# Spreading loads and preparation over the iterations, and moving TensorE transposes behind PV, in a fused attention and FFN kernel

## The chip, the cores and the metric

The kernel runs on one core of one Trainium2 chip. The metric is device microseconds (us) of one execution; a median of several runs is quoted with its range. A profile is one execution; its span, from the first to the last instruction, is about 1.8 us shorter than the time reported for the same run. Before the change the time was 451.42 us (median of 3 runs, 450.83 to 452.55).

## The reference, cut to what matters

```python
# q, k, v: [8, 8, 1152, 64]; two neighbouring queries are averaged: 576 rows
q_pool = q.reshape(B, H, S // 2, 2, D).mean(axis=3)
scores = np.matmul(q_pool, k.transpose(0, 1, 3, 2)) / np.sqrt(D)
attn   = softmax(scores)                       # over 1152 keys
x      = (attn @ v).transpose(0, 2, 1, 3).reshape(4608, 512)
out    = ((x @ w1) * (x @ w2)) @ w3 @ w_out    # d_ff = 1024
```

The kernel multiplies `w3 @ w_out` once, to a matrix T, and then runs the FFN in nine units of 512 tokens.

## The kernel before

Heads are handled in 32 *pairs*. A pair has 9 x 576 columns of scores, cut into chunks of 512 that run on across pairs; the loop makes two chunks in each of 162 *iterations*, so a pair takes 5.06 of them. In an iteration TensorE makes the scores of two chunks, ScalarE their exponentials, TensorE the products with v (PV) of the chunks before, and then *filler*: matmuls of T or of FFN units whose tokens are ready, until a running account (`busy`) of TensorE time reaches `due`. Two FFN units are left for a *tail* behind the loop.

Each pair has to be prepared: loads of k, q and v with a cast (queue of GpSimd), three copies on VectorE (pooled q, reordered k, v), and a transpose of k and q. The first eight pairs are transposed by TensorE, the others by DMA transposes, because in the beginning the DMA engines are full of loads.

```python
def load(P):      load_k(P); load_q(P); load_v(P)       # kst, vst: 4 buffers; qst: 3 pairs of two

def prep_stage(P):                                      # pairs 1 to 7, VectorE, in one go
    pool_q(P)
    kcs[P] = ab.tile(...); nc.vector.tensor_copy(out=kcs[P]..., in_=kst.pop(P))
    copy_v(P)

def prep_pe(P):                                         # 18 transposes, two PSUM tiles of tag "ff"
    t2 = psum.tile([128, 1024], FP16, tag="ff", bufs=2); t1 = psum.tile(..., tag="ff", bufs=2)
    ...                                                 # q and k[8] into t2, k[0..7] into t1
    nc.vector.tensor_copy(out=qT[P]..., in_=t2[:, 128:704])
    if P == 0: nc.scalar.copy(out=kT[P][:, 0:8]..., in_=t1)
    else:      nc.vector.tensor_copy(out=kT[P][:, 0:8]..., in_=t1)
    nc.vector.tensor_copy(out=kT[P][:, 8], in_=t2[:, 0:128])

def prep_dma(P):                                        # pairs 8 to 31: k, its transpose,
    ...                                                 # q, its transpose, v: in one go

def normalize(P):                                       # frees po, which has ONE buffer
    acc = po.pop(P)...; nc.vector.reciprocal(...); nc.vector.tensor_tensor(out=xn, ...)
    nc.sync.dma_start_transpose(out=xT..., in_=xn...)

load_q(0); load_k(0); ...; load_v(0); load(1); load(2)
load_w3(0); load_w(wosb, moe_w_out); load(3); load_w3(1)
...
for it in range(162):
    if it in T_AT: filler.append(gen_T(...))            # T_AT = (8, 14)
    scores(2*it); expo(2*it); scores(2*it+1); expo(2*it+1)
    at = it * 2 * CH / PAIR                             # position, in pairs
    if staged < 8 and at >= staged - 0.8:
        prep_stage(staged); ...                         # and one or two of the loads that wait
    if prepped < 32 and at >= prepped - (0.5 if prepped < 8 else 1.6):
        if prepped < 8: fill(0, settle=True); prep_pe(prepped)
        else:           prep_dma(prepped); load(loaded); ...
    for J, i in ready: attend(J, i)                     # PV
    if last: normalize(...)
    fill(due)
```

`settle=True` finishes the open accumulation group of the filler, because transposes and filler share the two `ff` tiles.

The softmax here doesn't subtract the row's maximum and nothing guards it: scores larger than these inputs give would overflow.

Of the kernel before, what the change touches and what calls it, by code (L numbers as in the profile page):

```python
# [8 lines left out]
FP16 = mybir.dt.float16  # L9
# [6 lines left out]
NJ = 9  # L16
# [7 lines left out]
def kernel(  # L24
# [11 lines left out]
    nc = tc.nc  # L36
    B, H, S, D = q.shape
# [5 lines left out]
    NP = B * H // 2  # L43
    SCL = 16.0
    NPE = 8
    T_AT = (8, 14)

    T_MM, T_TR, T_SC, T_AV = 0.216, 0.06, 0.63, 0.061
    PACE0, PACE1 = 2.2, 2.19
    SCALE = 0.5 * float(D) ** -0.5  # L50

# [2 lines left out]
    ab = ctx.enter_context(tc.tile_pool(name="ab", bufs=4))  # L54
    ffp = ctx.enter_context(tc.tile_pool(name="ffp", bufs=2))
    psum = ctx.enter_context(
        tc.tile_pool(name="psum", bufs=1, space=bass.MemoryType.PSUM))

    xT = const.tile([128, NC, NT], FP16)
    w1sb = const.tile([128, NC, dff], FP16)  # L60
    w2sb = const.tile([128, NC, dff], FP16)
# [6 lines left out]
    ident = const.tile([128, 128], FP16)  # L68
# [7 lines left out]
    kst, vst, qst, kT, qT, qps = {}, {}, {}, {}, {}, {}  # L76

    def load_q(P):
        if P % 2 == 0:
            qst[P // 2] = stage.tile([128, 2, 18, D], FP16, tag="qst", bufs=3, name="qst")  # L80
        b, h0 = P // 4, 2 * (P % 4)
        o = 64 * (P % 2)
        nc.gpsimd.dma_start(
            out=qst[P // 2][o:o + 64].rearrange("p u t d -> p u (t d)"),
            in_=q[b, h0:h0 + 2].rearrange("u (p t) d -> p u (t d)", t=18))

    def load_k(P):
        b, h0 = P // 4, 2 * (P % 4)
        kst[P] = stage.tile([128, 2, NJ, D], FP16, tag="kst", name="kst")
        nc.gpsimd.dma_start(  # L90
            out=kst[P].rearrange("p u j d -> p u (j d)"),
            in_=k[b, h0:h0 + 2].rearrange("u (p j) d -> p u (j d)", j=NJ))

    def load_v(P):
        b, h0 = P // 4, 2 * (P % 4)
        vst[P] = stage.tile([128, 2, NJ, D], FP16, tag="vst", name="vst")
        nc.gpsimd.dma_start(  # L97
            out=vst[P].rearrange("p u j d -> p u (j d)"),
            in_=v[b, h0:h0 + 2].rearrange("u (p j) d -> p u (j d)", j=NJ))

    def load(P):
        if P < NP:
            load_k(P)
            load_q(P)
            load_v(P)

    def pool_q(P):

        pp, o = P // 2, 64 * (P % 2)
        if P % 2 == 0:  # L110
            qps[pp] = ab.tile([128, NJ, 2, D], FP16, tag="qp", bufs=2, name="qp")
        if P < NPE:
            r = slice(o, o + 64)
        elif P % 2 == 0:
            r = slice(0, 128)
        else:
            return
        src = qst[pp][r].rearrange("p u (c two) d -> p u c two d", two=2)
        nc.vector.tensor_tensor(
            out=qps[pp][r].rearrange("p c u d -> p u c d"),  # L120
            in0=src[:, :, :, 0, :], in1=src[:, :, :, 1, :], op=ALU.add)

    def new_kq(P):
        kT[P] = ab.tile([128, NJ, 128], FP16, tag="kT", bufs=3, name="kT")
        qT[P] = ab.tile([128, NJ, 64], FP16, tag="qT", bufs=3, name="qT")

    def copy_v(P):
        nc.vector.tensor_copy(out=vts[P % 4][:, :, :, 0:D], in_=vst.pop(P))

    def prep_dma(P):  # L130

        pp, o = P // 2, 64 * (P % 2)
        new_kq(P)
        kc = ab.tile([128, NJ, 2, D], FP16, tag="kc", bufs=2, name="kc")
        nc.vector.tensor_copy(out=kc.rearrange("p j u d -> p u j d"), in_=kst.pop(P))  # L135
        nc.sync.dma_start_transpose(out=kT[P], in_=kc.rearrange("p j u d -> p (j u d)"))
        pool_q(P)
        nc.sync.dma_start_transpose(
            out=qT[P], in_=qps[pp][o:o + 64].rearrange("p c u d -> p (c u d)"))
        copy_v(P)  # L140

    kcs = {}

    def prep_stage(P):

        pool_q(P)
        kcs[P] = ab.tile([128, NJ, 2, D], FP16, tag="kc", bufs=2, name="kc")
        nc.vector.tensor_copy(out=kcs[P].rearrange("p j u d -> p u j d"), in_=kst.pop(P))
        copy_v(P)

    def prep_pe(P):
        pp, o = P // 2, 64 * (P % 2)
        new_kq(P)
        kc = kcs.pop(P)
        t2 = psum.tile([128, 1024], FP16, tag="ff", bufs=2, name="t2")
        t1 = psum.tile([128, 1024], FP16, tag="ff", bufs=2, name="t1")
        for c in range(NJ):
            nc.tensor.transpose(t2[:, 128 + 64 * c:192 + 64 * c],
                                qps[pp][o:o + 64, c].rearrange("p u d -> p (u d)"),
                                ident[o:o + 64, o:o + 64])  # L160
        for j in (8, 0, 1, 2, 3, 4, 5, 6, 7):
            dst = t1[:, 128 * j:128 * j + 128] if j < 8 else t2[:, 0:128]
            nc.tensor.transpose(dst, kc[:, j].rearrange("p u d -> p (u d)"), ident)
        nc.vector.tensor_copy(out=qT[P].rearrange("p c f -> p (c f)"), in_=t2[:, 128:704])
        if P == 0:
            nc.scalar.copy(out=kT[P][:, 0:8].rearrange("p j f -> p (j f)"), in_=t1)
        else:
            nc.vector.tensor_copy(out=kT[P][:, 0:8].rearrange("p j f -> p (j f)"), in_=t1)  # L168
        nc.vector.tensor_copy(out=kT[P][:, 8], in_=t2[:, 0:128])


    psc = {}
# [60 lines left out]
    def load_w3(i):  # L233
        t = ffp.tile([128, 4, dff], FP16, tag="g", name="w3h")
        nc.gpsimd.dma_start(
            out=t, in_=moe_w3.rearrange("(c p) f -> p c f", p=128)[:, 4 * i:4 * i + 4])
        w3h.append(t)

    def load_w(dst, src):
        nc.gpsimd.dma_start(out=dst, in_=src.rearrange("(c p) f -> p c f", p=128))  # L240
# [31 lines left out]
    def gen_ffn(t, tail):  # L272
# [25 lines left out]
        for i in range(4):  # L298
# [13 lines left out]
            for s in range(2):  # L312
# [13 lines left out]
        out=ident, in_=ident, compare_op=ALU.not_equal, fill=1.0,  # L326
        base=0, channel_multiplier=1, pattern=[[-1, 128]])
    load_v(0)
    load(1)
    load(2)  # L330
    load_w3(0)
    load_w(wosb, moe_w_out)
    load(3)
    load_w3(1)
    waiting = [lambda: load(4), lambda: load_w(w1sb, moe_w1), lambda: load_w(w2sb, moe_w2),
               lambda: load(5), lambda: load(6)]
    loaded, staged, prepped = 7, 1, 1
    prep_stage(0)
    prep_pe(0)

    n_units = NT // 512
    filler = []
    next_unit = 0
    busy = due = 0.0
# [4 lines left out]
    def fill(until, settle=False):  # L349

        nonlocal busy, whole
        while filler and (not whole if settle else busy < until):
            try:
                cost, whole = next(filler[0])
                busy += cost
            except StopIteration:
                filler.pop(0)

    for it in range(NIT):
        if it in T_AT:  # L360
            filler.append(gen_T(T_AT.index(it)))

        while next_unit < n_units:
            last_b = (512 * (next_unit + 1) - 1) // SQ
            if (last_b + 1) * 4 * PAIR + 3 * 2 * CH > it * 2 * CH:
                break
            filler.append(gen_ffn(next_unit, False))
            next_unit += 1
        scores(2 * it)
        expo(2 * it)  # L370
        scores(2 * it + 1)
        expo(2 * it + 1)
        busy += T_SC
        due = (due if filler else busy - T_SC) + (PACE0 if it < 20 else PACE1)
        at = it * 2 * CH / PAIR
        if staged < NPE and at >= staged - 0.8:
            prep_stage(staged)
            staged += 1
            if waiting:
                waiting.pop(0)()  # L380
                if waiting:
                    waiting.pop(0)()
            else:
                load(loaded)
                loaded += 1
        lead = 0.5 if prepped < NPE else 1.6
        if prepped < NP and at >= prepped - lead:
            if prepped < NPE:
                fill(0, settle=True)
                prep_pe(prepped)  # L390
            else:
                prep_dma(prepped)
                load(loaded)
                loaded += 1
            prepped += 1
        ready = [b for b in blocks[nb:nb + 40]
                 if b[0] * SQ + min(128 * b[1] + 128, SQ) <= 2 * it * CH]

        last = [n for n, (J, i) in enumerate(ready) if J % NJ == NJ - 1 and i == 4]
        if last:  # L400
            ready = ready[:last[0] + 1]
        busy += T_AV * len(ready)
        for J, i in ready:
            attend(J, i)
        if last:
            normalize(ready[-1][0] // NJ)
        nb += len(ready)
        fill(due)
    for J, i in blocks[nb:]:
        attend(J, i)  # L410
    normalize(NP - 1)
# [37 lines left out]
```

## Time and profile before

| | before |
|---|---|
| time, median of 3 runs | 451.42 us |
| span of the profiled execution | 446.9 us |
| TensorE / ScalarE / VectorE busy | 94% / 74% / 44% |
| iterations 0-7, 41-160: us each | 2.0, 2.27 |
| iteration 40 | 8.34 us |
| TensorE idle in iteration 40 | 4.73 us |

The start of an iteration is read as the start of its first exponential (324 exponentials, two for each iteration). The page's first part (engine: us busy, share of the span, instructions) and a line of its fourth (the chain of work that ended last):

```profile
PE 418.3 (94%) x5168; PEld 222.5 (50%) x5168; DVE 198.2 (44%) x347; ACT 329.8 (74%) x350; POOL 69.9 (16%) x107
...
PE 82%; DMA 5%; ACT 4%; DVE 4%; issue 3%; SPq 1%; POOL 0%; ACTq 0%; DVEq 0%; POOLq 0%
```

TensorE (PE) is the limit almost everywhere. The stretches of 10 us show where it is not: each line has the busy time and the instructions of each engine, the granted TensorE clock (the share of full speed that TensorE was allowed), the mean busy share of the DMA engines, and what they moved. The busy share adds up the time of all packets and divides it by 16 engines; over 1, packets overlap on an engine.

```profile
core 0: us, PE busy (x) PEld busy (x) DVE busy (x) ACT busy (x) POOL busy (x), PEclk, DMA share, GB/s
10.00:20.00 10.00, 8.37 (x123) 5.45 (x123) 2.96 (x7) 8.62 (x10) 4.29 (x7) 1.00 1.16 207
20.00:30.00 10.00, 7.57 (x137) 5.45 (x137) 4.64 (x10) 8.30 (x9) 1.47 (x2) 1.00 1.27 204
100.00:110.00 10.00, 10.00 (x126) 5.06 (x124) 4.56 (x9) 8.76 (x10) 2.03 (x3) 1.00 1.39 126
110.00:120.00 10.00, 5.27 (x49) 2.54 (x49) 1.15 (x3) 3.38 (x5) 0.00 (x0) 0.83 1.25 131
200.00:210.00 10.00, 9.97 (x143) 5.45 (x140) 3.82 (x8) 8.60 (x9) 2.03 (x3) 1.00 0.73 104
```

The last line is the steady state: TensorE without a gap, ScalarE (ACT) at 8.6 of 10 us. From 110 to 120 us TensorE loses almost half its time and part of its clock. The timeline of TensorE there (start, us, engine, line, operation, out<-in, count, and in brackets the idle time before it with what ended it):

```profile
109.91 0.39 PE L187 MATMUL psc<-qT,kT 64*128 64x512 f16 x2
115.03 0.61 PE L187 MATMUL psc<-qT,kT 64*128 64x512 f16 x2 [4.73 <-DMA qT<-qp]
```

and the line of the chain of waits for the same place (start, us, what):

```profile
98.94 15.96 DMA qT<-qp
```

The scores of pair 8, the first that is transposed by DMA, wait for its q. That transpose was issued at 98.94 us and took 15.96 us to land. The trace's clock record has 0.5 of the full clock for 3.41 us from 114.64 on.

### The profile page before, as it was taken

The numbers are of one execution on the slowest core, as the hardware profiler recorded it, in microseconds if no ns is written. First come the engines' busy times: TensorE is split into PE (matmuls) and PEld (weight loads), VectorE is DVE, ScalarE is ACT, GpSimd is POOL, SyncE is SP. The second block draws the span as 40 slices with busy tenths as digits, with TensorE's granted clock in tenths as the row PEclk, the third lists the DMA queues.
The fourth block names the chain that finished last, engine by engine and source line by source line (L and its number), as shares of the span: only waits on it lengthen the run. The fifth ranks groups of instructions, "written<-read, shape, count | busy, mean of one in ns | idle before, by whom it ended". The sixth has DMA issues, their size and how long they took to land.

```text
span 446.9 us, 12036 instructions
## 1 busy us (share of the span) xinstructions
PE 418.3 (94%) x5168; PEld 222.5 (50%) x5168; DVE 198.2 (44%) x347; ACT 329.8 (74%) x350; POOL 69.9 (16%) x107
## 2 busy tenths in 40 slices
PE   2889898998799999999999999999999999989995
PEld 1556454554355555555555555545555555544442
DVE  2245454574234553554445445544554444433130
ACT  2977776778488888888888888878888888823332
POOL 7312140131101121111111111111100000000000
PEclk9999999999899999999999999999999999999999
DMA  8999999669999999999899999979882460131304
GB/s 132 209 188 206 207 183 194 100 99 122 135 196 141 136 135 223 135 155 117 163 169 130 142 175 166 137 110 182 163 151 56 98 101 19 15 73 36 92 4 94
DMA packets 94468, 59.11 MB, mean 132 GB/s; under 512 B 66256, under 2 KB 83664, under 8 KB 94416
## 3 DMA queue, kind: packets, MB, share of 16 engines
q0 software_dynamic: 25168, 33.56, 50.4%
q1 hardware_dynamic: 69248, 24.79, 37.3%
q8 instruction: 40, 0.66, 0.6%
q14 instruction: 12, 0.10, 0.1%
HBM read 67.11 MB, written 9.44 MB: 171 GB/s over the span
## 4 chain that ended last, share of the span: by engine, by line
PE 82%; DMA 5%; ACT 4%; DVE 4%; issue 3%; SPq 1%; POOL 0%; ACTq 0%; DVEq 0%; POOLq 0%
PE po L206 20%; PE psc L187 19%; PE pb L291 13%; PE pa L278 13%; PE pp L301 12%; ACT er L193 4%; DMA qT<-qp 4%; PE pT L265 3%; DMA vst<-in_v_dram 1%; DVE xn L218 1%; DVE kT L168 1%; PE w3t L250 1%; DMA out_dram<-osb 1%; DVE T_73 L269 0%; DVE osb L310 0%
## 5 line engine op out<-in xcount | busy, mean ns | idle before, releaser
L193 ACT ACTIVATE er<-psc 128x1024 f16<-128x1024 f32 x324 | 313.4, 1022 | 70.8 <-PE psc L187 68.0
L187 PE MATMUL psc<-qT,kT 64*128 64x512 f16 (+7 forms) x1152 | 108.8, 289 | 11.3 <-DMA qT<-qp 4.7
L206 PEld LDWEIGHTS <-er 128*128 128x128 f16 x2880 | 97.3, 97 | 35.1 <-issue 31.8
L187 PEld LDWEIGHTS <-kT 64*128 64x128 f16 x1152 | 44.2, 94 | 95.4 <-issue 83.7
L291 PE MATMUL pb<-xT,w2sb 128*128 128x512 f16 x288 | 79.7, 379 | 2.4 <-DVE osb L310 1.3
L278 PE MATMUL pa<-xT,w1sb 128*128 128x512 f16 x288 | 79.1, 379 | 1.2 <-DVE asb L287 0.7
L296 DVE TENSOR_TENSOR gT<-pb,asb 128x512 f16<-128x512 f32 x72 | 49.6, 689 | 63.5 <-PE pb L291 63.0
L301 PE MATMUL pp<-T_73,gT 128*128 128x512 f16 x288 | 70.8, 382 | 0.0
L287 DVE COPY asb<-pa 128x512 f32<-128x512 f32 x56 | 38.5, 688 | 46.9 <-PE pa L278 46.9
L90 POOL DMA_DIRECT2D kst<-in_k_dram x32 | 23.0, 718 | 217.1 <-DVE kc L135 173.3
L310 DVE TENSOR_SCALAR osb<-pp 128x512 f32<-128x512 f32 x28 | 19.3, 690 | 53.5 <-PE pp L301 51.1
L301 PEld LDWEIGHTS <-gT 128*128 128x128 f16 x288 | 25.5, 98 | 24.4 <-issue 0.5
L278 PEld LDWEIGHTS <-w1sb 128*128 128x128 f16 x288 | 25.8, 97 | 23.8 <-issue 0.7
L291 PEld LDWEIGHTS <-w2sb 128*128 128x128 f16 x288 | 25.4, 97 | 23.6 <-issue 1.6
L206 PE MATMUL po<-vt_77,er 128*128 128x65 f16 x720 | 29.7, 195 | 0.0
L206 PE MATMUL po<-vt_80,er 128*128 128x65 f16 x720 | 29.4, 195 | 0.1
L206 PE MATMUL po<-vt_78,er 128*128 128x65 f16 x720 | 28.7, 193 | 0.0
L206 PE MATMUL po<-vt_79,er 128*128 128x65 f16 x720 | 28.7, 193 | 0.0
L285 ACT COPY asb<-pa 128x512 f32<-128x512 f32 x16 | 9.4, 586 | 24.4 <-PE pa L278 24.4
L218 DVE TENSOR_TENSOR xn<-po,rz 128x640 f16<-128x640 f32 x32 | 26.4, 824 | 1.3 <-DVE rz L216 0.2
L97 POOL DMA_DIRECT2D vst<-in_v_dram x32 | 23.3, 729 | 17.4 <-DMA w3h<-in_moe_w_dram 5.3
L216 DVE RECIPROCAL rz<-po 128x10 f32<-128x10 f32 x32 | 7.1, 221 | 37.6 <-PE po L206 37.5
(80 smaller groups left out, 147.7 us busy)
## 6 DMA issues: line engine op xcount, KB each, us to landing
qst<-in_q_dram POOLq DMA_DIRECT2D x32, 288.0 KB, 7.8
kst<-in_k_dram POOLq DMA_DIRECT2D x32, 288.0 KB, 5.5
vst<-in_v_dram POOLq DMA_DIRECT2D x32, 288.0 KB, 9.4
out_dram<-osb SPq DMA_DIRECT2D x72, 128.0 KB, 3.4
w3h<-in_moe_w_dram POOLq DMA_DIRECT2D x2, 1024.0 KB, 20.4
wosb<-in_moe_w_out_dram POOLq DMA_DIRECT2D x1, 1024.0 KB, 19.2
xT<-xn SPq DMA_TRANSPOSE x64, 3.8
w1sb<-in_moe_w_dram POOLq DMA_DIRECT2D x1, 1024.0 KB, 21.6
```

Of the source, the lines that this page charges most:

```text
L90: nc.gpsimd.dma_start(out=kst[P].rearrange("p u j d -> p u (j d)"), in_=k[b, h0:h0 + 2].rearrange("u (p j) d -> p u (j d)", j=NJ))
L97: nc.gpsimd.dma_start(out=vst[P].rearrange("p u j d -> p u (j d)"), in_=v[b, h0:h0 + 2].rearrange("u (p j) d -> p u (j d)", j=NJ))
L187: nc.tensor.matmul(t[:, u, o:o + ln], kT[P][s, j, :], qv[s, f0:f0 + ln], start=True, stop=True)
L193: nc.scalar.activation(out=er[:, :, r:r + CH], in_=psc.pop(c), func=AF.Exp, bias=0.0, scale=SCALE)
L206: nc.tensor.matmul(po[P][:, u, VW * i:VW * i + D + 1], er[:, u, r:r + 128], vts[P % 4][:, u, j, 0:D + 1], start=(j == 0 and i == 0), stop= ...
L218: nc.vector.tensor_tensor(out=xn.rearrange("p i u d -> p u i d"), in0=acc[:, :, :, 0:D], in1=rz.to_broadcast([128, 2, 5, D]), op=ALU.mult)
L278: nc.tensor.matmul(pa, w1sb[:, mc, ft * 128:ft * 128 + 128], xT[:, mc, t0:t0 + 512], start=(mc == 0), stop=(mc == NC - 1))
L287: nc.vector.tensor_copy(out=asb, in_=pa)
L291: nc.tensor.matmul(pb, w2sb[:, mc, ft * 128:ft * 128 + 128], xT[:, mc, t0:t0 + 512], start=(mc == 0), stop=(mc == NC - 1))
L296: nc.vector.tensor_mul(out=gT[:, ft, :], in0=pb, in1=asb)
L301: nc.tensor.matmul(pp, gT[:, ft, 128 * i:128 * i + 128], T16[:, ft, :], start=(ft == 0), stop=(ft == NF - 1))
L310: nc.vector.tensor_scalar_mul(out=osb, in0=pp, scalar1=1.0 / (SCL * SCL))
```

## The change

Its intent: loads one pair at a time, each at its own position; VectorE's three copies of a pair one for each iteration and earlier (1.3 pairs ahead instead of 0.8; for DMA pairs 1.8 instead of 1.6); TensorE's transposes behind PV, charged to the account; T one iteration earlier; pair 0's kT copied by two engines. Cut to its core:

```diff
-    T_AT = (8, 14)
-    T_MM, T_TR, T_SC, T_AV = 0.216, 0.06, 0.63, 0.061
+    T_AT = (7, 13)
+    T_MM, T_TR, T_SC, T_AV = 0.216, 0.042, 0.63, 0.061
...
         if P == 0:
-            nc.scalar.copy(out=kT[P][:, 0:8]..., in_=t1)
+            nc.scalar.copy(out=kTP[:, 512:1024], in_=t1[:, 512:1024])
+            nc.vector.tensor_copy(out=kTP[:, 0:512], in_=t1[:, 0:512])
...
     load(1)
-    load(2)
     load_w3(0)
     load_w(wosb, moe_w_out)
-    load(3)
+    load(2)
     load_w3(1)
-    waiting = [...]
-    prep_stage(0)
-    prep_pe(0)
+    loads = [(0.4, load 3), (0.4, load 4), (1.0, w1), (1.0, w2), (2.0, load 5), ...]  # P at P - 3.0
+    pool_q(0); copy_k(0); pe_kq(0); copy_v(0)
...
-        due = ... + (PACE0 if it < 20 else PACE1)
+        due = ... + (PACE0 if it < 40 else PACE1)
-        if staged < NPE and at >= staged - 0.8:
-            prep_stage(staged); ...
-        lead = 0.5 if prepped < NPE else 1.6
-        if prepped < NP and at >= prepped - lead: ...      # prep_pe or prep_dma, and a load
+        while loads and at >= loads[0][0]:
+            loads.pop(0)[1]()
+        if staged < NP and at >= staged - (1.3 if staged < NPE else 1.8):
+            side += [pool_q(P), copy_k(P)] if staged < NPE else [dma_k(P), dma_q(P)]
+            side.append(copy_v(P))
         ...                                              # PV, normalize
+        if prep_now:
+            pe_kq(prepped); busy += 18 * T_TR; prepped += 1
         fill(due)
+        if side and not last:
+            side.pop(0)()
+        prep_now = prepped < NPE and at >= prepped - 0.7 and prepped in kcs
+        if prep_now: fill(0, settle=True)
```

More of the change, by code (lines that the diff above doesn't have):

```diff
@@ L128, in copy_v, with copy_k, dma_k, dma_q @@
         nc.vector.tensor_copy(out=vts[P % 4][:, :, :, 0:D], in_=vst.pop(P))
-    def prep_dma(P):
-        pp, o = P // 2, 64 * (P % 2)
-        new_kq(P)
-        kc = ab.tile([128, NJ, 2, D], FP16, tag="kc", bufs=2, name="kc")
-        nc.vector.tensor_copy(out=kc.rearrange("p j u d -> p u j d"), in_=kst.pop(P))
-        nc.sync.dma_start_transpose(out=kT[P], in_=kc.rearrange("p j u d -> p (j u d)"))
-        pool_q(P)
-        nc.sync.dma_start_transpose(
-            out=qT[P], in_=qps[pp][o:o + 64].rearrange("p c u d -> p (c u d)"))
-        copy_v(P)
     kcs = {}
-    def prep_stage(P):
-        pool_q(P)
+    def copy_k(P):
         kcs[P] = ab.tile([128, NJ, 2, D], FP16, tag="kc", bufs=2, name="kc")
         nc.vector.tensor_copy(out=kcs[P].rearrange("p j u d -> p u j d"), in_=kst.pop(P))
-        copy_v(P)
-    def prep_pe(P):
+    def dma_k(P):
+        new_kq(P)
+        copy_k(P)
+        nc.sync.dma_start_transpose(
+            out=kT[P], in_=kcs.pop(P).rearrange("p j u d -> p (j u d)"))
+    def dma_q(P):
+        pool_q(P)
+        o = 64 * (P % 2)
+        nc.sync.dma_start_transpose(
+            out=qT[P], in_=qps[P // 2][o:o + 64].rearrange("p c u d -> p (c u d)"))
+    def pe_kq(P):
         pp, o = P // 2, 64 * (P % 2)
@@ L155, in prep_pe @@
         t2 = psum.tile([128, 1024], FP16, tag="ff", bufs=2, name="t2")
-        t1 = psum.tile([128, 1024], FP16, tag="ff", bufs=2, name="t1")
         for c in range(NJ):
@@ L160, in prep_pe @@
                                 ident[o:o + 64, o:o + 64])
-        for j in (8, 0, 1, 2, 3, 4, 5, 6, 7):
-            dst = t1[:, 128 * j:128 * j + 128] if j < 8 else t2[:, 0:128]
-            nc.tensor.transpose(dst, kc[:, j].rearrange("p u d -> p (u d)"), ident)
+        nc.tensor.transpose(t2[:, 0:128], kc[:, 8].rearrange("p u d -> p (u d)"), ident)
+        t1 = psum.tile([128, 1024], FP16, tag="ff", bufs=2, name="t1")
+        for j in range(8):
+            nc.tensor.transpose(t1[:, 128 * j:128 * j + 128],
+                                kc[:, j].rearrange("p u d -> p (u d)"), ident)
         nc.vector.tensor_copy(out=qT[P].rearrange("p c f -> p (c f)"), in_=t2[:, 128:704])
+        kTP = kT[P].rearrange("p j f -> p (j f)")
         if P == 0:
-            nc.scalar.copy(out=kT[P][:, 0:8].rearrange("p j f -> p (j f)"), in_=t1)
-        else:
-            nc.vector.tensor_copy(out=kT[P][:, 0:8].rearrange("p j f -> p (j f)"), in_=t1)
-        nc.vector.tensor_copy(out=kT[P][:, 8], in_=t2[:, 0:128])
+            nc.scalar.copy(out=kTP[:, 512:1024], in_=t1[:, 512:1024])
+            nc.vector.tensor_copy(out=kTP[:, 0:512], in_=t1[:, 0:512])
+        else:
+            nc.vector.tensor_copy(out=kTP[:, 0:1024], in_=t1)
+        nc.vector.tensor_copy(out=kTP[:, 1024:1152], in_=t2[:, 0:128])
     psc = {}
@@ L329 @@
     load(1)
-    load(2)
     load_w3(0)
     load_w(wosb, moe_w_out)
-    load(3)
+    load(2)
     load_w3(1)
-    waiting = [lambda: load(4), lambda: load_w(w1sb, moe_w1), lambda: load_w(w2sb, moe_w2),
-               lambda: load(5), lambda: load(6)]
-    loaded, staged, prepped = 7, 1, 1
-    prep_stage(0)
-    prep_pe(0)
+    loads = [(0.4, lambda: load(3)), (0.4, lambda: load(4)),
+             (1.0, lambda: load_w(w1sb, moe_w1)), (1.0, lambda: load_w(w2sb, moe_w2)),
+             (2.0, lambda: load(5)), (3.0, lambda: load(6)), (4.0, lambda: load(7))]
+    loads += [(P - 3.0, lambda P=P: load(P)) for P in range(8, NP)]
+    staged, prepped = 1, 1
+    side = []
+    prep_now = False
+    pool_q(0)
+    copy_k(0)
+    pe_kq(0)
+    copy_v(0)
     n_units = NT // 512
@@ L373 @@
         busy += T_SC
-        due = (due if filler else busy - T_SC) + (PACE0 if it < 20 else PACE1)
+        due = (due if filler else busy - T_SC) + (PACE0 if it < 40 else PACE1)
         at = it * 2 * CH / PAIR
-        if staged < NPE and at >= staged - 0.8:
-            prep_stage(staged)
-            staged += 1
-            if waiting:
-                waiting.pop(0)()
-                if waiting:
-                    waiting.pop(0)()
-            else:
-                load(loaded)
-                loaded += 1
-        lead = 0.5 if prepped < NPE else 1.6
-        if prepped < NP and at >= prepped - lead:
-            if prepped < NPE:
-                fill(0, settle=True)
-                prep_pe(prepped)
-            else:
-                prep_dma(prepped)
-                load(loaded)
-                loaded += 1
-            prepped += 1
+        while loads and at >= loads[0][0]:
+            loads.pop(0)[1]()
+        if staged < NP and at >= staged - (1.3 if staged < NPE else 1.8):
+            if staged < NPE:
+                side += [lambda P=staged: pool_q(P), lambda P=staged: copy_k(P)]
+            else:
+                side += [lambda P=staged: dma_k(P), lambda P=staged: dma_q(P)]
+            side.append(lambda P=staged: copy_v(P))
+            staged += 1
         ready = [b for b in blocks[nb:nb + 40]
@@ L407 @@
         nb += len(ready)
+        if prep_now:
+            pe_kq(prepped)
+            busy += 18 * T_TR
+            prepped += 1
         fill(due)
+        if side and not last:
+            side.pop(0)()
+        prep_now = prepped < NPE and at >= prepped - 0.7 and prepped in kcs
+        if prep_now:
+            fill(0, settle=True)
     for J, i in blocks[nb:]:
```

## The prediction

> **What bounds the kernel now.** The page gives TensorE 94%, ScalarE 74%, VectorE 44%. The chain of waits is 82% TensorE, 5% DMA. Reading the exponentials (L193) as a clock for the 162 iterations: iterations 0-7 take 2.04 us each (two exponentials of about 1 us: ScalarE is the limit, there is no filler), iterations from 41 on take 2.27 us with TensorE at 9.97 of 10 us in the stretches (TensorE is the limit). Three things stand out above this floor:
> - the six iterations with TensorE preparation after the first ones take 3.4 to 4.5 us. The 18 transposes are about 1.3 us of true TensorE work; stretches from 30 to 100 us show TensorE idle 3.9 us in all;
> - iteration 40 takes 8.34 us: qT of pair 8, the first made by DMA transpose, is issued at 98.94 and lands at 114.90. TensorE is idle 4.7 us and the granted clock is then 0.5 for 3.4 us (about 1.7 us more). The Trainium skill, "TensorE: Matmul & The Clock Gate", Part 1, says that an idle window of about 3.4 us halves the clock; this trace agrees;
> - the first exponential starts at 10.58 us.
>
> **What the change does not do.** Loads wait for buffers, not for their place in the loop: the waits view shows GpSimd waiting 173 us for VectorE's copies that free kst. The new positions hardly matter once buffers are full; the order does.
>
> **Gains.**
> 1. Start: copy_v after the transposes, kT of pair 0 split: about 1 us.
> 2. Iteration 40: kT of pair 8 is issued one iteration earlier, with fewer loads in the same stretch (vst later, the next load not at once). kT issue to qT landing took 11 to 13 us in later pairs; there are about 14 us now. Mostly gone: -5 us.
> 3. Transposes behind PV: banks are evacuated meanwhile. Of 3.9 us idle, -2.5. The 0.756 us now charged per preparation shortens these iterations, but moves filler to the tail (32 matmuls left instead of 25 by my count, +1.5 us): work moved, not removed.
> 4. Small stalls by VectorE lumps at 223 and 292 us, filler starting one iteration earlier: -1.
>
> **Loss.** Loads of pair 2 now stand behind w3's first half and w_out. Transfers of the GpSimd queue landed in order: v1 13.58, k2 15.47, q2 16.46, v2 17.84, w3h 23.44, w_out 28.56. With the two weights (10.7 us) in front, q2 should land near 27 us, k2 near 26. But VectorE is now asked for pool_q(2) in iteration 4, at about 19 us, half a pair earlier than before, and works in order: it blocks until 27, so normalize(0) ends near 29.4 instead of 24.4. There is one po buffer, so PV of pair 1 and all behind it on TensorE wait about 5 us, perhaps with the clock halved after it (+1). Later loads (pairs 3, 5) then arrive about when asked for.
>
> **Sum.** -1 -5 -2.5 -1 +1.5 +5 and about +1: 451.4 to about 448; I say 447.5. Range 440 to 454. Chances: faster 0.17, same 0.79, slower 0.04.
>
> **What would show it.** The exponentials: first at 9.6 us; a gap of 4 to 6 us near iteration 7 with VectorE idle before qp, released by the DMA of qst, at about 19 to 27 us; preparation iterations under 3.2 us; no gap over 1 us at pair 8; 2.27 us per iteration after.
>
> **What would make it wrong.** q2 landing before 22 us (then about 442, faster possible); pair 8's transposes still landing late, as loads and transposes share the DMA engines (the skill, "DMA: Bandwidth & Descriptors", section "Issuing engines are not separate DMA queues"; here the DMA share is 1.39 at 100 to 110 us), then about 453; VectorE blocking again on pairs 3 or 5, +2 us each.

## The result, and the profile after

The changed kernel takes **446.09 us** (median of 4 runs, 445.76 to 446.78); the kernel before took 451.14 us beside it (450.83 to 452.55). The ratio is 0.9884, interval 0.9859 to 0.9909: same within 2%, and 1.2% faster beyond noise. A ratio is the mean time of one kernel's fast runs over the mean time of the other's of the same rounds, so not quite the ratio of the medians.

The stretches that answer to those of before:

```profile
10.00:20.00 10.00, 8.20 (x119) 5.05 (x120) 3.64 (x9) 8.10 (x9) 2.85 (x5) 1.00 1.15 206
20.00:30.00 10.00, 3.66 (x59) 2.17 (x56) 2.08 (x4) 6.88 (x8) 2.84 (x4) 0.78 1.18 209
30.00:40.00 10.00, 9.66 (x140) 6.81 (x139) 4.37 (x9) 3.88 (x4) 2.04 (x3) 0.88 1.22 186
100.00:110.00 10.00, 10.00 (x138) 5.34 (x135) 5.69 (x12) 8.77 (x10) 3.36 (x5) 1.00 1.07 171
110.00:120.00 10.00, 9.94 (x128) 5.12 (x128) 4.25 (x8) 8.35 (x9) 2.04 (x3) 1.00 1.06 143
200.00:210.00 10.00, 9.97 (x122) 5.03 (x120) 4.18 (x7) 8.67 (x10) 2.04 (x3) 1.00 1.04 147
```

The hole at 110 us is gone: TensorE no longer idles in front of pair 8's first scores (timeline of TensorE):

```profile
112.83 0.60 PE L188 MATMUL psc<-qT,kT 64*128 64x512 f16 x4
```

A new hole stands at 20 to 30 us, with a reduced clock in it and behind it. The chain of waits from 18 to 36 us tells what it is (start, us, what):

```profile
8.28 19.26 DMA qst<-in_q_dram
...
27.56 0.04 DVE qp L119
...
28.85 0.84 DVE xn L219
29.68 0.05 issue
29.73 2.05 PE po L207 x34
```

and the waits view (engine, line, waited for: us in total, times, longest):

```profile
DVE qp L119 <- DMA qst<-in_q_dram: 13.4, 3, 7.6
PE po L207 <- DVE xn L219: 4.2, 1, 4.2
```

q of pair 2 is issued at 8.28 us, lands at 27.54; VectorE (DVE) stands 7.6 us in front of pooling it, and behind that pooling, in order, stands normalize(0) (`xn`), which frees the one `po` tile for the PV of pair 1. TensorE waits 4.2 us.

I cut both traces into segments by the exponentials. All in us; "idle" is TensorE's idle time before its instructions there, gaps over 50 ns:

```
segment               before (idle)   after (idle)   difference
start to exponential 0   10.58           10.90          +0.32
iterations 0 to 9        22.76 (4.06)    29.36 (8.19)   +6.60
iterations 10 to 39      77.06 (3.81)    73.07 (2.96)   -3.99
iteration 40              8.34 (4.73)     2.27 (0.00)   -6.07
iterations 41 to 160    272.96 (1.23)   272.94 (1.17)   -0.02
tail                     55.23 (1.40)    55.38 (0.00)   +0.15
span                    446.93          443.92          -3.01
```

The medians differ by 5.05 us, the two traces by 3.01. The kernel before varies: its profiled run took 448.69 us at a mean clock of 0.995, most of its other runs 450.3 to 452.7 at 0.991 to 0.992. One more half-clock stretch of 3.4 us would lower a mean clock by about 0.004; that fits, but those runs have no trace, so it is argued and not shown.

### The profile page after: what moved, and what is told of

It is laid out like the page before. It is cut to its first block, busy times and chain, and to the rows that moved or that the text cites. A ratio compares the mean times of both kernels' runs of the same rounds, so it can differ in the third digit from the quotient of the medians.

```text
span 443.9 us, 12036 instructions
## 1 busy us (share of the span) xinstructions
PE 417.9 (94%) x5168; PEld 222.7 (50%) x5168; DVE 197.2 (44%) x348; ACT 329.4 (74%) x350; POOL 69.9 (16%) x107
## 4 chain that ended last, share of the span: by engine, by line
PE 88%; DMA 4%; DVE 2%; issue 2%; POOL 2%; ACT 2%; ACTq 0%; POOLq 0%
PE po L207 22%; PE psc L188 20%; PE pb L292 14%; PE pa L279 13%; PE pp L302 13%; DMA qst<-in_q_dram 4%; PE pT L266 3%; ACT er L194 1%; PE w3t L251 1%; POOL kst L90 0%; DVE xn L219 0%; DVE T_73 L270 0%; DVE kT L169 0%; POOL vst L97 0%; POOL qst L83 0%
## 5 line engine op out<-in xcount | busy, mean ns | idle before, releaser
L302 PE MATMUL pp<-T_73,gT 128*128 128x512 f16 x288 | 69.9, 379 | 0.0
L119 DVE TENSOR_TENSOR qp<-qst 128x1152 f16<-128x1152 f16 (+1 forms) x20 | 15.0, 749 | 13.5 <-DMA qst<-in_q_dram 13.4
## 6 DMA issues: line engine op xcount, KB each, us to landing
w3h<-in_moe_w_dram POOLq DMA_DIRECT2D x2, 1024.0 KB, 17.6
```

What stands on the lines that cost most here:

```text
L302: nc.tensor.matmul(pp, gT[:, ft, 128 * i:128 * i + 128], T16[:, ft, :], start=(ft == 0), stop=(ft == NF - 1))
```

## The experiments

Twelve kernels ran, in three jobs of four, each job beside seven runs of the kernel before on its own chip. In the first job one of those seven took 442.96 us at clock 1.000, the others 450.3 to 452.7 at 0.992; by the rule of 1.5% above the fastest that labels the six "slow". It leaves one fast run to compare with, so I quote no ratio of that job, and compare e1 and e3 with the changed kernel's four fast runs. (442.96 is about what the kernel before takes when the stall in iteration 40 is removed, see e7; that the stall sometimes fails to come is likely, but no trace of that run exists.)

Segments of every trace, as above; "k to scores" is from the landing of pair 0's k to the first scores, because that landing itself varied from 6.6 to 8.7 us whatever the kernel:

```
                        k to    first  it 0-9  it 10-39   it 40  it 41-160  tail    time, median
                        scores  exp                                                 (range)
before                   3.16   10.58   22.76    77.06     8.34    272.96   55.23   451.42
changed                  2.82   10.90   29.36    73.07     2.27    272.94   55.38   446.09 (445.76-446.78)
e1_load2_first           2.82   11.98   23.85    74.21     2.27    273.72   55.39   442.24 (441.56-443.28)
e2_before_load2_late     3.08   10.27   25.68    77.07     8.63    273.28   55.26   451.42 (450.60-453.56)
e3_ask_late              2.82   10.19   26.42    73.08     2.27    272.99   55.36   442.26 (441.84-442.44)
e4_vector_half_first     2.20   11.02   29.89    73.14     2.27    272.94   55.41   446.52 (one look)
e5_orders                2.20    9.52   30.42    73.14     2.27    272.99   55.36   443.47 (440.63-445.56)
e6_prep_before_pv        2.20   11.55   24.97    71.72     2.27    272.94   55.39   440.26 (439.58-440.70)
e7_before_stage7_early   2.79   11.76   24.10    76.91     2.06    273.17   55.22   443.40 (442.65-444.97)
e8_stage7_late           2.20   11.19   24.67    73.14    12.41    273.43   55.41   452.09 (one look)
e9_best                  2.20    9.50   26.53    74.96     5.62    275.64   57.31   448.71 (447.53-451.43)
e10_best_behind_pv       2.20   11.11   23.32    77.05     5.56    274.04   57.29   446.57 (445.81-450.20)
e11_best_lump            2.20   11.11   22.34    76.48     2.27    274.22   57.31   445.59 (445.47-446.08)
e12_best_no_charge       2.20    9.67   23.75    79.80     3.72    286.65   52.34   442.37, 442.64; slow 457.87, 462.53
```

### The new hole at the start: e1, e2, e3

**e1_load2_first.** The changed kernel with one order undone.

```diff
     load(1)
+    load(2)
     load_w3(0)
     load_w(wosb, moe_w_out)
-    load(2)
     load_w3(1)
```

> The changed kernel with one thing undone: the loads of pair 2 stand again in front of w3's first half and w_out. My theory (VectorE, in order, blocks on q of pair 2, which lands behind 2 MB of weights, and normalize(0) behind it holds the single po buffer): q of pair 2 lands near 16.5 us, VectorE waits under 1 us for it, iteration 7 falls from the 10.8 us of the changed kernel to about 4.5 us, no half clock; the time falls by 5 to 7 us to about 440. Rival (the early asking or the 10 filler items in iteration 7 make the long iteration, whatever the load order): iteration 7 stays over 8 us and the time within 1.5 us of 446.

q of pair 2 landed at 17.26 us, iteration 7 fell from 10.82 to 5.30 us, TensorE kept the full clock, and the time fell by 3.9 us to 442.24 (another chip; the kernel before took 451.14 us beside the one and 451.56 beside the other). The mechanism is as expected, the size a little under the 5 to 7 us. The trace shows two reasons: pair 0's k happened to land 1.1 us later than in the changed kernel's trace, and pair 3's q, at 38.31 us, now made VectorE wait 2.85 us and TensorE 0.98 us behind it.

**e2_before_load2_late.** The kernel before with that order alone.

```diff
     load(1)
-    load(2)
     load_w3(0)
     load_w(wosb, moe_w_out)
+    load(2)
     load(3)
```

> The kernel before with only this load order taken over: pair 2's loads behind w3's first half and w_out. It asks for pool_q(2) in iteration 7, at 24.3 us, after normalize(0). My theory: q lands near 27.5, VectorE waits about 3 us, but normalize(0) is already done, so only preparation 2 in iteration 8 waits, about 3 us: 453 to 455. Rival (the order alone makes the 10.8 us iteration): an iteration of over 8 us and 456 to 458.

VectorE asks for q after normalize(0) here. It waited 2.82 us and TensorE 1.25 us; iteration 8 took 7.45 instead of 4.54 us, no iteration 7 of 10.8 us came. So the order alone does not make the large hole. The time missed my figure: 451.42, within the scatter of the kernel before. The 2.9 us that iterations 0 to 9 lost are in the trace; in the time they cannot be told from the variation of iteration 40.

**e3_ask_late.** The changed kernel with its late loads, asked for later.

```diff
-        if staged < NP and at >= staged - (1.3 if staged < NPE else 1.8):
+        if staged < NP and at >= staged - (0.8 if staged == 2 else 1.3 if staged < NPE else 1.8):
```

> The changed kernel with its load order, but VectorE asked for pair 2 in iteration 7 instead of 4, behind normalize(0). My theory: VectorE still idles until q of pair 2 lands near 27.5, but normalize(0) ends near 25 us, PV of pair 1 does not wait, TensorE's idle time of 4.2 us and the half clock go; iteration 7 falls to under 6 us and the time to about 440 to 442. Rival (the data itself is needed that early, so late loads cost the same wherever they are waited for): the stall moves to preparation 2, and the time stays within 1.5 us of 446.

q of pair 2 still landed at 27.43 us. But normalize(0) ended near 24.5, PV of pair 1 started at 25.03 instead of 29.73, iteration 7 took 5.09 us, and the time is 442.26 us, the same as with the loads reordered. Together, e1 and e3 show that the hole needs both: a late load, and an in-order engine told to wait for it in front of the work that frees `po`. Either half removes it. Rival explanations that put it on early asking alone (e1), or on the late data alone (e3), fall. The lines of TensorE and VectorE, first e1 (normalize(0), PV of pair 1):

```profile
25.21 0.82 DVE L219 TENSOR_TENSOR xn<-po,rz 128x640 f16<-128x640 f32 x1
26.52 1.20 PE L207 MATMUL po<-vt,er 128*128 128x65 f16 x34
```

then e3, where pooling q of pair 2 comes last:

```profile
23.72 0.82 DVE L219 TENSOR_TENSOR xn<-po,rz 128x640 f16<-128x640 f32 x1
25.03 1.20 PE L207 MATMUL po<-vt,er 128*128 128x65 f16 x34
27.92 0.74 DVE L119 TENSOR_TENSOR qp<-qst 64x1152 f16<-64x1152 f16 x1
```

### The start of pair 0: e4

```diff
         if P == 0:
-            nc.scalar.copy(out=kTP[:, 512:1024], in_=t1[:, 512:1024])
             nc.vector.tensor_copy(out=kTP[:, 0:512], in_=t1[:, 0:512])
+            nc.scalar.copy(out=kTP[:, 512:1024], in_=t1[:, 512:1024])
```

> The changed kernel with the two halves of pair 0's kT copied in the other program order: VectorE's half first, ScalarE's second. In the changed kernel VectorE's half waited 1.01 us for ScalarE's (both read one PSUM tile). If the two are kept apart in program order, VectorE's half now starts near 9.1 us, and scores, which need that half alone for the first chunk, start near 9.6 instead of 10.25 us: first exponential 0.5 to 0.7 us earlier than 10.9. If the wait had another cause, it stays at 10.9. One look only: the time can't show so little.

In the changed kernel the two "parallel" halves ran one after the other: VectorE's copy waited for ScalarE's (waits view of the changed kernel).

```profile
DVE kT L167 <- ACT kT L166: 1.0, 1, 1.0
```

With the order exchanged, the wait is exchanged too (waits view of e4):

```profile
ACT kT L167 <- DVE kT L166: 8.3, 1, 8.3
```

(ScalarE had nothing else to do in those 8.3 us.) From k's landing to the first scores took 2.20 instead of 2.82 us, as expected. The first exponential did not come earlier, 11.02 us, because k landed 0.7 us later in this run. The Trainium skill, "PSUM — Partial Sum Buffer", section "PSUM bank collisions raise a hardware error", says that two engines may not touch one bank at the same time, reads included, and that access is to be guarded by bank and group of 32 partitions, or simply by bank; both halves are read from one tile of 2 KiB over all partitions, and the traces show a wait between them in either order. That agrees: 1.0 us of wait. By that page a split of columns between engines has to be a split between banks. The halves also have one destination tile, kT; that the wait is for the bank, and not for that tile, no run here shows.

### Placement of the transposes: e5, e6, e10

**e5_orders.** The changed kernel with loads of pairs 2 and 3 in front of the weights, and e4's order.

```diff
     load(1)
+    load(2)
     load_w3(0)
     load_w(wosb, moe_w_out)
-    load(2)
+    load(3)
     load_w3(1)
-    loads = [(0.4, lambda: load(3)), (0.4, lambda: load(4)),
+    loads = [(0.4, lambda: load(4)),
```

> The changed kernel with three orders mended: pair 2's loads in front of w3's first half and w_out, pair 3's loads in front of w3's second half (with pair 2 first alone, VectorE still waited 2.85 us for q of pair 3 and TensorE 0.98 us behind it), VectorE's half of pair 0's kT first (0.6 us from k's landing to the first scores). Theory: none of the three waits remains; first exponential to iteration 12 takes under 28.5 us (31.9 in the changed kernel's trace, 29.6 with pair 2 first alone); about 440.5 to 441.5, against 442.2 with pair 2 first alone. Rival (moving weights back only moves the wait to the T filler that needs them): iterations 7 to 14 get as much longer, 442 or more.

Half a miss. The time is 443.47 us with two runs at 445.5 and two near 441, and in the profiled one, a run of 445.56 us, iteration 7 takes 11.28 us again, for another reason:

```profile
25.11 1.05 PE L251 MATMUL w3t<-ident,w3h 128*128 128x128 f16 x16
30.59 3.57 PE L266 MATMUL pT<-wosb,w3T 128*128 128x512 f16 x8 [4.42 <-DMA wosb<-in_moe_w_out_dram]
```

Now w_out is late (30.45 us) for the T filler that the change starts in iteration 7. That is the rival: the wait moves to the user of the weights. From 10 to 30 us the DMA engines are full (a share of 1.15 to 1.27 in the stretches shown), so, as I read it, the order decides mostly who waits. In e6, where the first exponential came at 11.55 us and w_out at 28.68, this wait is not in the trace.

**e6_prep_before_pv.** e5_orders with the transposes in front of PV again, with their charge.

```diff
+        if prep_now:
+            pe_kq(prepped)
+            busy += 18 * T_TR
+            prepped += 1
         ready = [...]
         ...                        # PV, normalize
-        if prep_now:
-            pe_kq(prepped)
-            busy += 18 * T_TR
-            prepped += 1
         fill(due)
```

> The kernel of e5_orders with one part undone: the TensorE transposes in front of PV again, their charge of 0.756 us kept. Theory A (behind PV the PSUM banks are evacuated meanwhile, worth about 0.3 to 0.4 us in each of six preparations): about 2 us slower than e5_orders. Theory B (the shorter preparation iterations come from the charge alone, which moves filler): the same within 0.7 us.

Neither theory: it is *faster*. 440.26 us, ratio 0.9744 to the kernel before (0.9701 to 0.9787), the best of all kernels run. The starts of the two traces differ, so I read the placement from iterations 10 to 39 alone: 71.72 against 73.14 us, 1.42 us less. Both traces have the same 992 matmuls and transposes there, of the same kinds, so no filler moved in or out; TensorE's idle time makes 0.86 us of it (2.18 against 3.04). The timeline of TensorE in the preparation of pair 3 with the transposes behind PV (e5):

```profile
46.82 0.72 PE L207 MATMUL po<-vt,er 128*128 128x65 f16 x18
...
47.90 0.61 PE L161 MATMUL t<-ident,kc 128*128 128x128 f16 x8
49.36 0.38 PE L266 MATMUL pT<-wosb,w3T 128*128 128x512 f16 x1 [0.85 <-DVE kT L169]
```

and the same preparation with the transposes in front of PV (e6):

```profile
43.73 0.61 PE L161 MATMUL t<-ident,kc 128*128 128x128 f16 x8
44.17 0.71 PE L207 MATMUL po<-vt,er 128*128 128x65 f16 x18
45.19 0.38 PE L266 MATMUL pT<-wosb,w3T 128*128 128x512 f16 x1 [0.30 <-DVE kT L169]
```

The transposes fill both `ff` tiles, and the next filler matmul needs one of them. Behind PV nothing stands between, and TensorE waits 0.85 us for VectorE's copies. In front of PV, PV's 0.7 us cover most of it.

**e10_best_behind_pv.** The same comparison repeated on e9_best (below), with the edit of e6 reversed.

```diff
-        if prep_now: pe_kq(prepped); ...      # in front of PV
         ...                                   # PV, normalize
+        if prep_now: pe_kq(prepped); ...      # behind it
         fill(due)
```

> The kernel of e9_best with the TensorE transposes behind PV, as in the changed kernel: the clean form of the comparison e5 with e6, whose starts differed. Theory from those traces (behind PV the next user of the two ff banks, the filler, stands right after the transposes and waits 0.8 us for VectorE's three copies; in front of PV, PV covers that and 0.24 us are left): 1 to 1.6 us slower than e9_best, iterations 10 to 40 longer by about 1.4 us. Rival (my prediction's step: behind PV is the better place, by 2 us): faster than e9_best.

Iterations 10 to 39: 77.05 against 74.96 us, 2.09 us longer behind PV with the same TensorE work, 1.18 us of it idle time of TensorE. The segment agrees with e5 and e6. The whole times say the opposite, 446.57 against 448.71 us, and the intervals of their ratios to the kernel before overlap (0.9917 with 0.9855 to 0.9979; 0.9940 with 0.9882 to 0.9998): e9's trace lost 3.2 us more in iterations 0 to 9, most of it in a wait for w_out, and 1.6 us more in iterations 41 to 160. The verdict rests on the two pairs of segments, each of one trace; that the placement gains whole time is not shown.

### The hole at pair 8: e7, e8

**e7_before_stage7_early.** The kernel before with one number changed. VectorE's copy of pair 7's k frees the buffer into which pair 11's k is loaded; three iterations earlier, it moves pair 11's loads away from pair 12's, which start with pair 8's transposes.

```diff
-        if staged < NPE and at >= staged - 0.8:
+        if staged < NPE and at >= staged - (1.3 if staged == 7 else 0.8):
```

> The kernel before with one number changed: VectorE stages pair 7 in iteration 29 instead of 32. That frees kst for pair 11's loads some 6 us earlier, so these are done when pair 8's two DMA transposes are issued, which stay in iteration 34. Theory (the 17.3 us from issue of kT to landing of qT came from two pairs' loads, 11 and 12, at once on the shared DMA engines): it falls to 10 to 13 us, iteration 40 falls from 8.3 to under 4 us, and the time from about 451.5 to 444 to 446. Rival (pair 8 is simply asked for too late, whatever else is in flight): iteration 40 stays over 7 us and the time over 450.

**e8_stage7_late.** The reverse, on e5_orders: pair 7's three copies in iteration 32 in one piece. The transposes stay in iterations 33 and 34.

```diff
-        if staged < NP and at >= staged - (1.3 if staged < NPE else 1.8):
-            if staged < NPE:
+        if staged < NP and at >= staged - (0.8 if staged == 7 else 1.3 if staged < NPE else 1.8):
+            if staged == 7:
+                pool_q(7); copy_k(7); copy_v(7)
+            elif staged < NPE:
```

> The kernel of e5_orders with pair 7 staged on VectorE in iteration 32 in one piece, as in the kernel before, and pair 8's DMA transposes left in iterations 33 and 34. The reverse of e7: pair 11's loads now fall on pair 12's. Theory: from issue of kT(8) to landing of qT(8) takes over 11 us (7.5 in the changed kernel's trace), still inside the about 13 us that there are, so no long iteration or one under 4 us. Rival: the landing does not change (7 to 8.5 us). One look, for the landing times.

Issue and landing, us, as the traces have them:

```
                         v of pair 11      kT(8) issued    qT(8) landed    kT issued to   iteration 40
                         landed                                            qT landed
before                     101.71             97.58          114.90           17.3           8.34
e7 (spread)                 96.76             99.95          110.35           10.4           2.06
changed                    102.48            100.54          108.02            7.5           2.27
e8 (together again)        101.64             96.20          116.78           20.6          12.41
```

e7 removes the stall from the kernel before with one number: 443.40 us, ratio 0.9823 (0.9781 to 0.9865), with pair 8's own request left in iteration 34. e8, in its one run, brings it back to a kernel that had lost it. Pair 8's first scores in e7, then in e8 (timelines of TensorE):

```profile
112.28 0.60 PE L187 MATMUL psc<-qT,kT 64*128 64x512 f16 x4
...
116.91 0.61 PE L188 MATMUL psc<-qT,kT 64*128 64x512 f16 x2 [8.03 <-DMA qT<-qp]
```

I had expected e8's transposes to land late but still in time; the direction was right, the size too small (20.6 us, "over 11" in the text). The rival, that pair 8 is simply asked for too late, is refuted: kT(8) was issued 12.8 us before the start of iteration 40 in all four of these traces. What differs is how long the loads of pair 11 are still in flight when the transposes and the loads of pair 12 start. All of them share the DMA engines, as the Trainium skill says in "DMA: Bandwidth & Descriptors", section "Issuing engines are not separate DMA queues". But this is more than sharing, because less is moved in total. The stretch of e8 from 100 to 110 us, columns as before:

```profile
100.00:110.00 10.00, 8.89 (x117) 4.61 (x115) 5.27 (x10) 8.74 (x9) 2.29 (x4) 1.00 1.50 111
```

A busy share of 1.50 and 111 GB/s, where the changed kernel has 1.07 and 171 GB/s in the same stretch. Added up by queue from the packets, loads and transposes slow down alike: GpSimd's queue moved 76 instead of 110 GB/s, SyncE's, which has the transposes, 34 instead of 59.

The overlap is not the whole cause. I left out e12, whose trace is of a slow run, and looked at how long v of pair 11 was still in flight after kT(8) had been issued. Where it was 4.0 to 5.4 us (before, e2, e8, e9), qT(8) landed 16.7 to 20.6 us after kT was issued; where it was at most 2.4 us (changed, e1, e4, e5, e7, e11), 7.5 to 10.4 us. But at 2.5 to 2.8 us both occur: 7.4 and 7.6 us in e3 and e6, 17.6 us in e10. e3 and e10 issued kT, pair 12's loads and qT within 0.8 us of each other, and from 100 to 110 us the DMA engines moved 156 GB/s in e3 and 89 in e10. What else slows them is open.

### Three on the rest: e9, e11, e12

**e9_best.** e6_prep_before_pv with `T_AT = (8, 14)` instead of `(7, 13)`, to keep the T filler from waiting for w_out.

```diff
-    T_AT = (7, 13)
+    T_AT = (8, 14)
```

> The kernel of e6_prep_before_pv with T_AT back at (8, 14). In e5's trace the T filler that starts in iteration 7 stood 4.4 us waiting for w_out, which lands at 28.6 to 30.5 us when pair 2's loads go first; in iteration 8 the preparation of pair 2 stands in front of it. Theory: the wait is under 1 us, no half clock near 30 us; 438.5 to 439.5, runs within 1 us of each other. Rival (the start is bound by the loads' bandwidth anyway and the wait only moves): 440 or more.

A clear miss: 448.71 us, ratio 0.9940 (0.9882 to 0.9998). w_out landed at 31.23 us and TensorE still waited 2.95 us for it. Beside that, iterations 10 to 39 grew by 3.2 us, the tail by 1.9 us (T starts one iteration later, so more is left at the end), iterations 41 to 160 by 2.7 us, and pair 8's q came 2.2 us too late again, though kT(8) was issued 14.7 us before iteration 40: in this trace pair 11's v landed at 100.75, 4.5 us after kT(8) had been issued at 96.30. So these runs speak for starting T in iteration 7, and the positions of loads and transposes hold by small margins. Of the 3.2 us in iterations 10 to 39, 2.9 us are idle time of TensorE (5.06 against 2.18 us in e6), most of it in waits for VectorE's evacuations and for ScalarE; which part of the edit brings them I have not isolated.

**e11_best_lump.** e9_best with the pieces of a pair in one go.

```diff
-        if side and not last:
+        while side and not last:
             side.pop(0)()
```

> The kernel of e9_best with VectorE's three pieces of a pair issued one after the other in the same iteration, not one for each iteration. Theory (VectorE is under half busy, the pieces take 0.45 to 0.75 us each, and the time comes from the loads' spacing, not from the pieces): the same within 0.8 us. Rival (a lump of 1.7 us in front of the filler's evacuations stops TensorE once in each of 31 pairs): 3 us or more slower.

445.59 us, 3.1 us *less* than e9_best, so my "same within 0.8 us" was missed. In its trace iteration 40 is 2.27 us: the lump issues pair 8's kT 17.4 us before iteration 40 instead of 14.7, and its q right behind. Without iterations 0 to 9 and 40, the rest of the loop is 0.1 us longer than e9's: 1.52 us more in iterations 10 to 39, 1.42 us less in 41 to 160. The rival, a cost of 3 us or more, is refuted. That single pieces gain anything by themselves is not shown.

**e12_best_no_charge.** e9_best without the account's charge for transposes.

```diff
             pe_kq(prepped)
-            busy += 18 * T_TR
             prepped += 1
```

> The kernel of e9_best without the charge of 0.756 us of filler for each TensorE preparation. Theory (work moved, not removed: TensorE is the limit in these iterations and in the tail alike): iterations 10 to 40 longer by 2.5 to 4 us, the tail behind the last exponential shorter by about as much, the time the same within 0.8 us. Rival (the charge is a gain of its own, because it keeps ScalarE fed): 2 to 4 us slower.

Inconclusive in time: two runs at 442.4 and 442.6 us, two slow at 457.9 and 462.5, ratio of the fast ones 0.9811 (0.9739 to 0.9883). The trace is of a slow one (a DMA transpose of xT arrived late), so its loop is not used. Its tail is a matter of counts: 52.34 against 57.31 us, 5.0 us shorter. The six charges of 0.756 us that fall where there is filler (pairs 2 to 7) make 4.5 us, and filler comes in whole matmuls and groups: about this much had moved from the loop to the tail. The fast runs being 6 us below e9_best is not explained.

## Why the prediction was right

The time, 446.09 us, is 1.4 us under the 447.5 predicted, inside 440 to 454, and the class "same" had 0.79. Step by step, as it put them:

1. **Start, "about 1 us": wrong.** From k's landing to the first scores only 0.34 us were gained, and the first exponential came 0.32 us later, because k landed later. The step that failed is that the two halves of kT would be copied in parallel; they lie in one bank and were copied in turn (e4). Even in the better order it is 0.96 us from the kernel before (3.16 to 2.20).
2. **Iteration 40, "-5 us": right, a little under-sized.** -6.07 us in the traces. The reason given first, kT "issued one iteration earlier", did not come about: kT was issued 12.8 us before iteration 40 in both kernels. The second one, fewer loads in the same stretch, is what e7 and e8 support, as far as it goes (e3 against e10).
3. **"Transposes behind PV ... -2.5": the mechanism is wrong.** Iterations 10 to 39 did become 3.99 us shorter. But placing the transposes behind PV costs 1.4 to 2.1 us there (e5 and e6, e9 and e10), because it uncovers the evacuation of the transposes' own tiles. Already in the two traces TensorE's wait for that evacuation (VectorE's copy of kT) grew there, from 0.77 to 1.56 us. What shortened them is mostly moved work: they hold 11 matmuls (3 of T, 8 of the FFN) and 8 transposes of w3 less. At the account's 0.216 us for a matmul and 0.066 us for a transpose (16 of w3 took 1.05 us in e5) I estimate 2.9 us. The part of T moved to iterations 0 to 9, and the tail has 8 matmuls more. TensorE's idle time fell by 0.85 us in all. "32 matmuls left instead of 25" was exact: the timelines at the loop's end show 25 and 32 matmuls of one FFN unit. The 1.5 us that they cost were paid back, since a wait of 1.27 us behind them disappeared.
4. **"Small stalls by VectorE lumps at 223 and 292 us ... -1": not so.** Iterations 41 to 160 are unchanged, 272.96 and 272.94 us, with 1.23 and 1.17 us idle. The same step's "filler starting one iteration earlier" moved the part of T named in 3.
5. **The loss, "+5 and about +1": the mechanism is right, the size too large.** Undoing either half of it saved 3.9 us (e1) and 3.8 us (e3). q was predicted near 27 us and landed at 27.54; normalize(0) near 29.4, it ended at 29.67; TensorE idle 4.2 us and the clock at 0.5 for 6.8 us; iterations 0 to 9 +6.60 us, about 1.2 us of which is T work done earlier. The half clock is not the hole's alone: it began at 25.59 us, as the gap began (25.50), and e6 and e7 have 3.41 us of it at 24.95 and 26.70 us without the hole. The landing could be worked out because the transfers of GpSimd's queue landed in the order in which they were issued. The Trainium skill, "DMA: Bandwidth & Descriptors", section "Two DMAs through the same engine are not ordered", says that descriptors of one queue start in order, but that this is no guarantee of completion; for the loads issued in the first 35 us, landing order was issue order in all 14 traces. "q2 landing before 22 us (then about 442" was met by e1: 17.26 us and 442.24.

That the number came so close is luck. The terms as written (-1 -5 -2.5 -1 +1.5 +5 +1) add up to -2.0 us, so to 449.4; the prediction wrote "about 448" and then 447.5, without a term for the difference. Its own sum was 3.3 us too high. And errors cancelled: gains that did not come as meant (start, transposes, small stalls) stood against a gain that was under-sized (iteration 40) and costs that were over-sized (the loss, the matmuls left for the tail).

## What to carry to other kernels

Ask of each instruction that is moved earlier whether its data will be there: an in-order engine that waits for a load also holds everything behind it, and here that was the one buffer which TensorE needed next. In a stretch where the DMA engines are full, look who waits next when you change the order of loads (pair 2's q, then w_out in e5). Look also at what is in flight when a DMA transpose is issued: the same pair took 7.4 to 20.6 us here. Try work that fills all PSUM buffers in front of work that needs none of them, so that the evacuation is covered; here that saved 1.4 and 2.1 us in the stretch where it happens.

## What the Trainium skill lacked or had wrong

- "Advanced Engine Details and Errata", section "X-Bar Transpose (TRN2)": "TRN2 transpose DMAs are as fast as regular DMAs". Alone this agrees (kT 3.1 us from issue to landing at 331 us with no loads; a load of k, as large in SBUF and cast from twice the bytes, 4.3 us at its best). Beside two pairs' casting loads, of which the section says nothing, both were slow: in the kernel before 11.9 us for kT and 16.0 us for qT, half its size, and 9.8 to 13.5 us for the loads of pair 12; in e8 15.9 and 18.3 us, and 13.1 to 15.0 us.
- "DMA: Bandwidth & Descriptors" says that queues interleave on the same engines; it has nothing on total throughput falling when transposes and loads overlap: 111 GB/s at a busy share of 1.50 (e8), 126 at 1.39 (before) and 89 at 1.43 (e10), against 171 at 1.07 (changed) and 156 at 1.21 (e3), all from 100 to 110 us. The runs don't show why.
- "TensorE: Matmul & The Clock Gate", Part 1, says that an idle window of about 3.4 us halves the clock, and that these windows run freely, whatever the kernel does. The traces agree that the half clock comes in steps of that length: 3.41, 6.83 and 10.24 us. The page doesn't say how idle a window must be, or how long the half clock then lasts. A gap of 2.21 us was followed by 3.41 us of it (e9), one of 3.11 us by none (e10). In e7 it came for 3.41 us at 26.70 us though no gap in the 3.41 us before was over 0.52 us; TensorE was busy for 2.07 us of them. Gaps of 4.73 and 4.67 us (before, e2) gave 3.41 and 6.83 us.
